# A cluster-attention and spatial-gating kernel: a greedy order of instructions replaced by a fixed list for each engine

## The chip, the cores and the metric

The kernel runs on one core of one Trainium2 chip. The metric is the device time of one execution in microseconds (us), lower is better. Three runs of the kernel before took 635.9, 635.97 and 636.34 us; the median is 635.97.

A core has five engines that run side by side, each in its own program order: TensorE (PE in the rows; its weight loads are PEld), VectorE (DVE), ScalarE (ACT), GpSimd (POOL) and SyncE (SP), which issues most of the DMAs. An engine that waits for a semaphore holds up everything behind it in its own program; so the order in which the program lists the instructions of one engine is a decision of the kernel.

## The reference

Attention over four batches of eight heads, 768 positions of width 64, where a query sees only the keys of its own cluster, and then a gated MLP per batch:

```
q_assign = argmax(normalised q . normalised centroids)      # 16 clusters per head
k_assign = argmax(normalised k . normalised centroids)
scores   = where(q_assign == k_assign, q.k / 8, -1e9)
x        = softmax(scores) . v                              # 4 x 768 x 512
h        = relu(x @ w_in);  u, v = halves of h
v_n      = (v - mean) / sqrt(var + 1e-6)
v_s      = w_spatial @ v_n + b_spatial
out      = (u * v_s) @ w_out                                # 4 x 768 x 512
```

All of it is in float32; the kernel splits each float32 into a high and a low float16 and adds products of the parts.

## The kernel before, in words

**The work.** Heads are taken two at a time: 16 pairs n, four to a batch. For each pair, `prep` loads keys and queries (`raw`, L914) and values (`vraw`, L915), makes the high part on ACT (L918) and the low part `lo` on POOL after a scaled copy on ACT (L921, L922, pairs 1 to 3) or on DVE (L924), copies parts by DMA (L925, L926, L953), multiplies with the centroids on TensorE (the logits, L940 to L942) and finds the cluster by five DVE steps (L970 to L974); ACT writes the one-hot rows `ohx` (L983), a DMA transposes them (L987) and four DMAs put them into the operands (L999). `shifts` finds each query's largest score by nine score chunks on TensorE (L1041) and nine reductions on DVE (L1048), and writes the shift into the operands: by DMA (L1066, ACT L1067 and L1073, DMAs L1095 and L1096), or for the very first head through TensorE (L1083) and a DVE addition (L1089). `attend` makes scores (L1219, L1221), exponentials on ACT (L1226), a float16 cast (ACT L1241) and its remainder (POOL L1242), and sums values on TensorE (L1248). For eight of the heads (`turned`) the probabilities are transposed by DMA (L1163) before TensorE uses them (L1170 to L1172): 6 per head, 48 in all. Pair 0 has its own `prep0` (L834 to L890) with the row casts L890 shared by DVE and ACT. `raw` has one buffer: the load for a pair can be issued only when the low part of the pair before it has been made.

`mlp` runs once per batch: products in sub-groups of six matmuls of 512 columns (L1320), named V, U, S (spatial) and O (output). From S to O lead DVE L1397, ACT L1398, POOL L1399, a DMA transpose L1400; the output goes out by ACT L1417 and a DMA from ACT's queue (L1418). There are 24 such tiles. The weights are split in between (DVE L715, L730 to L732).

**The order.** Nothing is emitted where it is written. Every operation is recorded by `op` (L323) with its engine, an estimated cost and what it needs; `Plan.run` (L345) then plays a clock forward. Before the change it kept for each engine the operations whose inputs were done, took the engine that could start first, and on it the ready operation with the smallest due time; the due times, one number for each of 3355 operations, come from the table `STARTS` (L177). So an operation that is not ready in the planner's clock never stands in the way of one that is. What comes out is a fixed program for each engine.

```
                k = o.key if o.key >= FILLER else (g if o.due is None else o.due) + o.key
                if pick is None or (k, o.seq) < pick[:2]:
                    pick = (k, o.seq, o)
```

Of the kernel before, what the change touches and what calls it, by code (L numbers as in the profile page):

```python
# [17 lines left out]
P = 128  # L18
# [16 lines left out]
FILLER = 1e6  # L35
# [58 lines left out]
K_EXP = 17.89  # L94
# [34 lines left out]
K_FILL = -8.0  # L129
# [48 lines left out]
    "c-jrqgJK<65CG7bYs`z<v`K2)wr$(CZQHhO+qP}n_U`$IQx}>7K_bWiF(3urgea_xS@8!r2!hoR3eh1LqCq%>fB_G&Apmh;9lk_hiCJz|mt9B8LRfs(ktb!DSvxj>O=I!cHnx^MWAB;d6Int&fjwux*guw<$K<hi"  # L178
    "9$uVR;vab%UYNJ!ZFvvAnvda``Dgx{2aCx(u85`jsLiaF=*n}6vLdm#$2-eHVhHcgXN$h#vS=i3i^TH2xFjx!Qu3wPEQ-j+^0)XVmdobyh)kvS%S$q~DlJdQqN<hZuDYm!YKPh``>DZdh}x(&t8Qwm+Nt)a9_p^z"
    "rZ%Z9YL~jD52|Xg8!WbfmM{^@V0=UX$OU<!5EO+n5CM_EKtWZA1@#~uw1zgY7_Q<B<e;HERDjA*3+g}$NC*~ULNmw?W1ukHgGVq9Hoyaz0`0IDHisx^3vr<n#E15f06IfT=ntu&7o>sFkO?M0R>%okU?-G<>QE52"  # L180
    "!w#qfO&||+hhi`Y%E1sQ4x^w7jE9;q6KcR5XaKXI5iEf9a23wOMR*2bPy~`dGDr?3AuUvdvak>az-vei86gW~hHOwDYC}gD3?pDT41~!r9p*wqXbf*5E+)Xeun!KvE;s>);5ZzHvv3T~z-hP!=ioBjhD&fAPC{Sk"
    "15Y3b-$7IS0PXP$v_-_hsBt&~4#hB>jG;IOqvKNi4fU`I?uR>&9$P_9>;@&U2aJVAcnAAI9ejZmus77ip->fv!6fK|Pw+2vf!xpm@<BT&03~1~C@c+Af$$c527&2t8Z3q9umoPgN_YyNU=wt}pRfl8;9B?yYv3Pj"
    "1daxez%U$yiQxhyg&U9_?!!aK0c-Iw<cGuf7@y*6d<iMpABYFv;V4{zQ?MNF!aC>*0d%+(=fgZ$1S?<_Y=v!b5Prc|cmZ$VB;Lej@Bq`XaHiQmjKt&^4^v@m%#O)0GbX`&m=OzOCM<w?usmkN7B~@8V?wNjyRjhV"
    "!u(hr>tX|}ggvl6_QlpX1V`XVoQ2bI5>CK4$XS3L!5f$cJtoEwOpC!7150CLjD<C@6&Aw?%#AUz945t-*c`iIPiTV+uo*7HuDA_P<9?h02XHygh76bm^Wq3r4F_UF?2esr9CpM`xE}A~DBO#Wa4z=7`8Wnw;uKtk"
    "SMV9$$IUnz&)`%%i}P>^KEw}r5Z~ZO{Ef(nwPc-HC$<@m<9lHE4FpJ(PzwKIaSUTCa33DR6L<|<Vj)a~MX)Ru#gdo<YvVi2&yJyCbJ!xb7<=Ms9FMzjCT_xMcoY}nDcp(Ya1UO@9e4{b;XT}rYw$KkvQPLNgV-<p"
    "iQh3fi@_4H=qwqF&C;;KEC<WVO0d#wAv?m(vSDl<dxfdlTg<?|VnJ4fDYgj9GtV~QAFRS0tIi~=!y2);Yzt;%pRoY@f+g7xEXyjhSgZl7#uBh*tPAVQ2DAM9153|VuzYMiE6R4TeXIuS#m=xcY#=Mn4zUXCC~L|t"
    "u&b;a8^p%5RxB^;z{;>5tQ@Pv#<In%9-F~-u?=h^yT*dqVfKlI<2cqI$6^(%i0^R?i-y5GAxpw?vRbSy3uTN6R*Yp~X;~(AjNN4CSP0L})A6pXKdZ@7vBoS9Yr?X#)~pa~&nmKxtSTGInzP}oA)Cv(vwkcli(ucd"
    "6kE!cu_f#T+r)OW1MCL7!d|jd>;b#YzA(na_#5_z)n*s)GIE}Zk7j+?bk>_qWj)y#wv%0FQ`kXvhb>^E*h)5=tz$FUe0H8aVlUWU_K}@rKiFlacqo6uG>_zeSsb2-C*jF?C;pS&W58dr-|RIrJir~#z@zgho`rvB"
    "#F5A4g2&@&c`}}j7vV8@5Rc8H@x(j<Ps%g#`aBKK$(!=LyeKchck;p9@-n;uFUUKIq2eaL&FAvwyaPv}L<|ukqKh~pkw_>`@-sZMc*TG5y5bT4#0!gtqNRu?a*Imh6u-h7i;iNP_$h=8l?h}jnMLN8Ib<1GRaTTy"
# [118 lines left out]
class Plan:  # L308
# [36 lines left out]
    def run(self):  # L345
# [11 lines left out]
        for o in self.ops:  # L357
# [6 lines left out]
        wait = {e: [] for e in LAG}  # L364
        hw = [0.0, FIRST]
        count, nxt, fetch = 0, FETCH[0], []
        lanes = []
# [3 lines left out]
        def arm(o):  # L371
            o.ready = max([o.at] + [a.end + lag(a, o.eng) for a in o.after] + [a.s for a in o.order])
            wait[o.eng].append(o)
# [1118 lines left out]
```

## Time and profile before

| what | value |
| --- | --- |
| median of three runs | 635.97 us |
| the profiled execution: its span from the first to the last instruction | 633.5 us |
| what the median has beyond that span | 2.5 us |
| TensorE busy | 607.2 us, 96% of the span |
| VectorE, ScalarE, GpSimd busy | 409.4, 462.7, 440.1 us |
| mean granted TensorE clock | 0.989 |

The profile gives the profiled execution's time as its span; what lies around the span is not split further, and the table takes it as the difference to the median. Busy time is an average over stages with different limits: the stages have to be read one at a time. "nm<-acc" means that the instruction reads tile acc and writes tile nm; "x5" that five like it are merged; a bracket gives the idle time before an instruction and what ended it.

### The profile page before, as it was taken

The page shows a single profiled execution, that of the slowest core. Times are in us where ns is not written, and L with a number is a line of the kernel's source. Part 1 is how long each engine was busy: PE and PEld are TensorE (multiplying, and loading weights), DVE is VectorE, ACT ScalarE, POOL GpSimd, SP SyncE. Part 2 cuts the span into 40 slices and gives each one's busy share as a digit, 9 for nine tenths or more (in the row PEclk, how much of TensorE's full clock was granted, in tenths as well). Part 3 has the DMA queues.
Part 4 walks back from the last instruction along what each step waited for, and adds up shares of the span by engine and source line. Part 5 has one row for each costly group of instructions (what it writes and reads, how often), then busy time and mean ns, then how long its engine had stood idle before and what let it go on. Part 6 is the DMA issues. An engine that isn't in the chain of part 4 may idle for free.

```text
span 633.5 us, 16596 instructions
## 1 busy us (share of the span) xinstructions
PE 607.2 (96%) x6603; PEld 371.9 (59%) x6603; DVE 409.4 (65%) x856; ACT 462.7 (73%) x842; POOL 440.1 (69%) x377
## 2 busy tenths in 40 slices
PE   2799999999999999999999999999999999999997
PEld 1466777776666665456556655575556655444443
DVE  6969999998999978457777475478733551132110
ACT  5589999998998996539887978698877984133212
POOL 3386998988998995429988875588799966144120
PEclk9879999999999999999999999999999999999999
DMA  6467988966857748722899679995995199213133
GB/s 182 135 145 141 199 172 191 213 152 141 180 97 174 155 99 201 145 74 69 179 179 215 122 185 167 146 174 86 163 190 97 30 193 171 60 35 83 41 69 106
DMA packets 175171, 87.97 MB, mean 139 GB/s; under 512 B 159315, under 2 KB 162422, under 8 KB 175094
## 3 DMA queue, kind: packets, MB, share of 16 engines
q1 hardware_dynamic: 171350, 80.24, 63.1%
q10 hardware_dynamic: 3744, 6.69, 3.2%
q8 instruction: 51, 0.84, 0.6%
q14 instruction: 26, 0.21, 0.1%
HBM read 27.66 MB, written 6.29 MB: 54 GB/s over the span
## 4 chain that ended last, share of the span: by engine, by line
PE 73%; DVE 8%; ACT 7%; DMA 5%; POOL 3%; issue 3%; SPq 0%; ACTq 0%; POOLq 0%; DVEq 0%
PE acc L1320 39%; PE acc L1248 11%; PE acc L1219 5%; PE acc L1221 5%; PE acc L1041 5%; DVE nm L1048 3%; PE acc L1123 2%; PE acc L1121 2%; DMA pt<-pt 2%; DVE lo L924 1%; POOL pt L1162 1%; ACT p L1226 1%; ACT p L1152 1%; DMA raw<-in_kqT_dram 1%; PE acc L1170 1%
## 5 line engine op out<-in xcount | busy, mean ns | idle before, releaser
L1242 POOL TENSOR_TENSOR pt<-p,pt 128x768 f16<-128x768 f32 x136 | 226.4, 1686 | 34.2 <-ACT pt L1241 27.8
L1048 DVE TENSOR_REDUCE nm<-acc 128x1 f32<-128x512 f32 (+1 forms) x216 | 137.4, 681 | 13.2 <-PE acc L1041 12.7
L1226 ACT ACTIVATE p<-acc 128x512 f32<-128x512 f32 x216 | 120.7, 603 | 21.9 <-PE acc L1221 10.4
L1320 PE MATMUL acc<-win,xT 128*128 128x512 f16 x576 | 134.8, 379 | 0.3 <-ACT p L1152 0.3
L1241 ACT CAST pt<-p 128x768 f16<-128x768 f32 x136 | 110.4, 838 | 5.5 <-PE acc L1248 2.5
L1320 PE MATMUL acc<-vn,wsp 128*128 128x512 f16 x432 | 100.1, 379 | 0.4 <-ACT p L1152 0.4
L1162 POOL TENSOR_TENSOR pt<-p,pt 128x768 f16<-128x768 f32 x48 | 80.5, 1684 | 23.5 <-ACT pt L1161 17.5
L1248 PEld LDWEIGHTS <-pt 128*128 128x128 f16 x2448 | 87.5, 98 | 14.2 <-POOL pt L1242 1.5
L1248 PE MATMUL acc<-vhl,pt 128*128 128x65 f16 x2448 | 92.9, 193 | 1.0 <-POOL pt L1242 1.0
L1320 PEld LDWEIGHTS <-xT 128*128 128x128 f16 x576 | 54.4, 97 | 60.7 <-issue 0.8
L1219 PE MATMUL acc<-hq,lo 128*128 128x512 f16 (+1 forms) x288 | 84.0, 333 | 1.8 <-ACT p L1226 0.8
L1221 PE MATMUL acc<-hq 81*128 81x512 f16 (+1 forms) x288 | 84.2, 333 | 0.0
L1041 PE MATMUL acc<-hq 80*128 80x256 f16 (+1 forms) x288 | 71.8, 335 | 4.1 <-DVE nm L1048 1.6
L1320 PEld LDWEIGHTS <-wsp 128*128 128x128 f16 x432 | 41.1, 98 | 47.2 <-issue 0.9
L1152 ACT ACTIVATE p<-acc,bi,sl 128x512 f32<-128x512 f32 (+1 forms) x96 | 58.7, 679 | 10.6 <-DVE bi L1144 6.0
L1131 DVE TENSOR_REDUCE nm<-acc 128x1 f32<-128x512 f32 (+1 forms) x72 | 47.0, 684 | 23.0 <-PE acc L1123 22.8
L1399 POOL TENSOR_TENSOR ghl<-u,ghl 128x512 f16<-128x512 f32 x21 | 25.0, 1189 | 51.0 <-ACT ghl L1398 49.0
L1397 DVE SCALAR_TENSOR_TENSOR u<-acc,bsp,u 128x512 f32<-128x512 f32 x24 | 18.0, 749 | 65.5 <-PE acc L1320 65.3
L1320 PE MATMUL acc<-wou,gT 128*128 128x512 f16 x252 | 59.3, 379 | 0.5 <-ACT ohx L983 0.5
L1297 POOL TENSOR_TENSOR xhl<-xn,xhl 128x384 f16<-128x384 f32 x32 | 33.1, 1035 | 15.2 <-ACT xhl L1296 13.3
L1161 ACT CAST pt<-p 128x768 f16<-128x768 f32 x48 | 39.8, 840 | 4.1 <-DMA wraw<-pt 2.0
L1219 PEld LDWEIGHTS <-lo 128*128 128x128 f16 x288 | 28.0, 100 | 23.8 <-issue 4.0
(162 smaller groups left out, 1010.0 us busy)
## 6 DMA issues: line engine op xcount, KB each, us to landing
raw<-in_kqT_dram SPq DMA_DIRECT2D x15, 768.0 KB
vraw<-in_vp_dram SPq DMA_DIRECT2D x16, 384.0 KB
hq<-hq SPq DMA_DIRECT2D x15, 384.0 KB
out_dram<-o ACTq DMA_DIRECT2D x21, 256.0 KB
vn<-in_w_in_dram SPq DMA_DIRECT2D x8, 512.0 KB
hq<-lo SPq DMA_DIRECT2D x15, 192.0 KB
lo<-hq SPq DMA_DIRECT2D x15, 192.0 KB
wraw<-in_wsT_dram SPq DMA_DIRECT2D x12, 192.0 KB
```

The costliest lines, as they stand in the source:

```text
L1041: T.matmul(out=acc.t[:, c:c + cs.stop - cs.start], lhsT=hq.t[0:R_SH, 1, h, t * P:(t + 1) * P], rhs=hq.t[0:R_SH, 0, h, cs], start=c == 0, s ...
L1048: V.tensor_reduce(out=nm.t[:, t, k:k + 1] if n == 1 else nm.t[:, t:t + n, k], in_=src, axis=AX.X, op=ALU.max, negate=True)
L1131: V.tensor_reduce(out=nm.t[:, t, k:k + 1] if n_ == 1 else nm.t[:, t:t + n_, k], in_=src, axis=AX.X, op=ALU.max, negate=True)
L1152: A.activation(out=p32[j].t[:, halves[x]], in_=sc.t[:, j * (S - 512):(j + 1) * (S - 512)] if x else sc.t, func=AF.Exp, bias=bi.t[:, t:t + ...
L1162: c = op("POOL", 1.64, lambda pt=pt, j=j, p32=p32: G_.tensor_tensor(out=pt.t[:, S:], in0=p32[j].t, in1=pt.t[:, 0:S], op=ALU.subtract), aft ...
L1219: T.matmul(out=o, lhsT=lo.t[:, h, ks], rhs=hq.t[:, 2, h, cs], start=x == 0, stop=False, skip_group_check=True)
L1221: T.matmul(out=o, lhsT=hq.t[0:R_E, 0, h, ks], rhs=hq.t[0:R_E, 1, h, cs], start=False, stop=True, skip_group_check=True)
L1226: o = op("ACT", 0.6, lambda: A.activation(out=p32[j0].t[:, cs] if n_ == 1 else both(p32)[:, :, cs], in_=sc.t if n_ == 1 else sc.t.rearrang ...
L1241: o = op("DVE" if fast else "ACT", C_CAST if fast else 0.83, lambda pt=pt, p32t=p32t, fast=fast: (V.tensor_copy if fast else A.copy)(out=p ...
L1242: o = op("POOL", 1.64, lambda pt=pt, p32t=p32t: G_.tensor_tensor(out=pt.t[:, S:], in0=p32t(), in1=pt.t[:, 0:S], op=ALU.subtract), after=[o ...
L1248: T.matmul(out=a[:, c * W:c * W + w], lhsT=lhsT, rhs=rhs, skip_group_check=True, **f)
L1320: T.matmul(out=acc.t[:, 0:w], lhsT=lr[m][0], rhs=lr[m][1], start=(m == 0), stop=(m == n - 1))
```

## The change

The table `STARTS` is replaced, and with it what its numbers mean. The new one, unpacked, holds for every operation its place in its engine's list: 0 to 947 on TensorE, and in the same way for 867 operations on ACT, 837 on DVE, 361 on POOL and 342 on SP. `Plan.run` sorts each engine's operations by that number and only ever looks at the first of each list:

```
-            for e, q in wait.items():
-                first = None
-                for o in q:
-                    g = gate(o)
...
+        order = {e: sorted((o for o in self.ops if o.eng == e), key=lambda o: -o.due) for e in LAG}
+            for e, q in order.items():
+                if q and not q[-1].left:
+                    g = gate(q[-1])
+                    if g is not None and (best is None or max(g, free[e]) < best[0]):
+                        best = (max(g, free[e]), e)
...
-            wait[e].remove(o)
+            o = order[e].pop()
```

Five estimated costs change with it: the fill of two constants on DVE 1.2 to 0.42 (L636, the memsets of L633 and L634), two memset groups on POOL 2.0 to 0.8 (L641) and 0.8 to 0.4 (L644), and the exponentials of turned heads 0.6 and 0.4 to 0.78 and 0.57 (L1154). The operations, their operands and their number are unchanged.

By place, 832 of TensorE's 948 operations stand elsewhere (by 4.5 places in the mean), 760 of ACT's 867, 726 of DVE's 837, 251 of POOL's 361 and 289 of SP's 342. Unpacked, the start of the new lists against the old (h0 and h1 are the two heads of a pair, z0 and z1 the two parts of a row):

```
ACT old: ... L890 p0 h1z0, L918 p1 x2, L921 p1 x2, L890 h1z1, L775 v1, L815, L781 v1, L1067, L1073, L1067, L1073,
         L815, L918 p2, L983 x2, L1226, L921 p2, L918 p2, L1226, L921 p2, L1226, L1067, L1073, L1241, L1226 x3, ...
ACT new: ... L872 x2, L918 p1 x2, L921 p1 x2, L840, L775 v1, L890 h0z1, L890 h1z0, L1067, L890 h1z1, L1073, L815,
         L781 v1, L1067, L1073, L1226, L983 x2, L918 p2, L921 p2, L918 p2, L921 p2, L1226 x2, L1241, L1226 x2, ...
SP old:  L627, L628, L828 h1, L829, L841 h0, L842 h0, L841 h1, L914 p1, L842 h1, L857 h0, L915 p1, L857 h1, L925 p1,
         L817, L915 p2, L914 p2, L926 p1, ...
SP new:  L627, L828 h1, L628, L829, L914 p1, L842 h0, L915 p1, L857 h0, L925 p1, L842 h1, L841 h0, L914 p2, L817,
         L926 p1, L841 h1, L915 p2, L857 h1, ...
DVE new: ... L656, L839 h0, L839 h1, L669 x2, L633, L865, ... L1048 x3, L890 h1 x2, L1048 x3, L1066, L1048 x2, L970 c1,
         L1089, L971, L1066, L972, L973, L974, L816, L1048 x2, L1089, L1048 x6, L970 c2, ...
PE new:  ... the nine L1041 of head 0, the logits of pair 1, L1083, L1041 x2, the first L1219/L1221, ...
```

Two later places, and the end:

```
ACT near 86 us, old:  L1226, L1226, L1241, L1226, L775 v2, L1241, L1067, L1073, L781 v2, L1226, L1226, L1296, ...
ACT there, new:       L1226, L1226, L1241, L1226, L1226, L1241, L775 v2, L1067, L781 v2, L1226, L1226, L1296, ...
DVE near 180 us, old: L1294, L1048 x4, L924 p9, L715, L1048 x2, L924 p9, L1048 x4, ...
DVE there, new:       L1048 x2, L715, L924 p9, L1293, L1048 x2, L924 p9, L1048 x2, L1294, L1048, L715, L1048 x3, ...
PE at the end, old: S35 S35 S35 O31 O31 O34 O32 O34 O32 O33 O33 O35 O35
PE at the end, new: S35 O31 O31 S35 S35 O32 O32 O33 O33 O34 O34 O35 O35
```

## Rows read from the trace of the kernel before

**Rows 1.** The page: the span, and the chain that ended last, by engine

```profile
span 633.5 us, 16596 instructions
...
PE 73%; DVE 8%; ACT 7%; DMA 5%; POOL 3%; issue 3%; SPq 0%; ACTq 0%; POOLq 0%; DVEq 0%
```

**Rows 2.** Busy time by stage: from:to, length, engines, PEclk, DMA share, GB/s

```profile
0.00:20.00 20.00, 8.18 (x71) 5.33 (x72) 13.51 (x55) 12.61 (x22) 6.70 (x25) 1.00 0.57 163
20.00:30.00 10.00, 7.11 (x71) 4.62 (x70) 9.84 (x20) 3.05 (x9) 3.61 (x3) 0.83 0.52 162
30.00:40.00 10.00, 8.37 (x74) 5.20 (x74) 5.15 (x11) 9.88 (x21) 7.25 (x5) 0.51 0.55 116
40.00:150.00 110.00, 106.97 (x1590) 80.68 (x1588) 106.22 (x199) 103.92 (x199) 95.48 (x63) 1.00 0.80 172
150.00:540.00 390.00, 386.67 (x4382) 235.28 (x4380) 258.16 (x545) 310.15 (x555) 303.98 (x250) 1.00 0.74 146
300.00:350.00 50.00, 48.87 (x516) 28.79 (x515) 37.24 (x86) 42.01 (x77) 42.85 (x40) 1.00 1.00 193
```

**Rows 3.** ACT in order of time, 29 to 43 us

```profile
29.51 0.84 ACT L918 ACTIVATE hq<-raw 128x768 f16<-128x768 f32 x1 [2.98 <-DMA raw<-in_kqT_dram]
30.26 0.53 ACT L983 ACTIVATE ohx<-acc 128x192 f16<-128x192 f32 x2
30.68 0.60 ACT L1226 ACTIVATE p<-acc 128x512 f32<-128x512 f32 x1
...
33.10 0.86 ACT L921 ACTIVATE raw<-raw 128x768 f32<-128x768 f32 x1
...
42.52 1.58 ACT L918 ACTIVATE hq<-raw 128x768 f16<-128x768 f32 x2 [0.51 <-DMA raw<-in_kqT_dram]
```

**Rows 4.** DVE in order of time, 21 to 37 us

```profile
21.61 0.15 DVE L1066 TENSOR_REDUCE nl<-nm 128x4 f32<-128x12 f32 x1
...
24.78 0.69 DVE L1089 TENSOR_TENSOR hq<-acc,hq 19x512 f16<-19x512 f32 x1
...
27.74 0.57 DVE L974 TENSOR_TENSOR acc<-acc,m 128x384 f32<-128x384 f32 x1
...
36.81 0.56 DVE L970 TENSOR_REDUCE mx<-acc 128x24 f32<-128x384 f32 x1 [4.39 <-PE acc L942]
```

**Rows 5.** POOL in order of time: the low parts of pair 1

```profile
18.75 3.24 POOL L922 TENSOR_TENSOR lo<-raw,hq 128x768 f16<-128x768 f32 x2 [5.75 <-ACT raw L921]
```

**Rows 6.** SP's queue in order of time: when DMAs were issued

```profile
9.85 0.33 SPq L914 DMA_DIRECT2D raw<-in_kqT_dram  x1
10.23 0.46 SPq L842 DMA_DIRECT2D hq<-lo  x1
...
16.03 0.46 SPq L857 DMA_DIRECT2D lo<-hq  x1
...
22.31 0.37 SPq L914 DMA_DIRECT2D raw<-in_kqT_dram  x1
...
37.37 0.36 SPq L914 DMA_DIRECT2D raw<-in_kqT_dram  x1
```

**Rows 7.** The chain that ended last, near 86 us: start, us, what

```profile
86.43 0.75 ACT wou L781
...
87.39 0.47 ACT p L1226
```

**Rows 8.** DVE in order of time, near 180 us

```profile
179.62 2.04 DVE L924 SCALAR_TENSOR_TENSOR lo<-raw,hq 128x768 f16<-128x768 f32 x1
...
182.04 1.27 DVE L1048 TENSOR_REDUCE nm<-acc 128x1 f32<-128x512 f32 x2
```

**Rows 9.** TensorE's waits after 150 us: us in total, times, longest

```profile
PE acc L1170 <- DMA wraw<-pt: 0.6, 2, 0.4
```

**Rows 10.** The end: TensorE's last matmuls and ACT's last output

```profile
623.24 6.64 PE L1320 MATMUL acc<-wou,p 128*128 128x512 f16 x30
...
630.06 0.60 ACT L1417 ACTIVATE o<-acc 128x512 f32<-128x512 f32 x1 [1.12 <-DMA out_dram<-o]
```

More of the change, by code (lines that the diff above doesn't have):

```diff
@@ L220 @@
[L220 to L222 removed]
+    "c-keH1)P*s7sgM((n~B2OLzCu-QBR%(y2&yDj^}=ASK-)5=x6oBM3-0NP~nl-+$&~emnENH%>nHoaZ89q7o_zCGbxrhPXtN=!`mlfu|70VoEG#UE(nkSBlFdnJm*~jLepbvQU=F3YjMxq^4|_9kQSA!%|-k%5QQ+cFPHgl"
@@ L363, in run @@
         free = {"PE": 0.6, "ACT": 1.1, "DVE": 0.63, "POOL": 0.57, "SP": 0.5, "NONE": 0.0}
-        wait = {e: [] for e in LAG}
         hw = [0.0, FIRST]
@@ L372, in arm @@
             o.ready = max([o.at] + [a.end + lag(a, o.eng) for a in o.after] + [a.s for a in o.order])
-            wait[o.eng].append(o)
         def gate(o):
@@ L394, in run @@
         done = 0
+        order = {e: sorted((o for o in self.ops if o.eng == e), key=lambda o: -o.due) for e in LAG}
         while done < len(self.ops):
             best = None
-            for e, q in wait.items():
-                first = None
-                for o in q:
-                    g = gate(o)
-                    if g is not None and (first is None or g < first):
-                        first = g
-                if first is not None:
-                    s = max(first, free[e])
-                    if best is None or s < best[0]:
-                        best = (s, e)
+            for e, q in order.items():
[3 more added lines that the diff above has]
+                        best = (max(g, free[e]), e)
             if best is None:
-                raise RuntimeError("the plan can't go on: " + str([(o.seq, o.eng) for q in wait.values() for o in q][:20]))
+                raise RuntimeError("the plan can't go on: " + str([(q[-1].seq, q[-1].eng) for q in order.values() if q]))
             s, e = best
-            pick = None
-            for o in wait[e]:
-                g = gate(o)
-                if g is None or g > s + 1e-9:
-                    continue
-                k = o.key if o.key >= FILLER else (g if o.due is None else o.due) + o.key
-                if pick is None or (k, o.seq) < pick[:2]:
-                    pick = (k, o.seq, o)
-            o = pick[2]
-            wait[e].remove(o)
+            o = order[e].pop()
             for tok in o.new:
@@ L634, in fill @@
         V.memset(ones, 1.0)
-    c_wt = op("DVE", 1.2, fill, key=K_FILL)
+    c_wt = op("DVE", 0.42, fill, key=K_FILL)
     c_id = op("DVE", 0.2, lambda: V.tensor_copy(out=id16, in_=idt()), after=[ld_i], use=[scratch], key=0)
@@ L1152, in ex @@
                         A.activation(out=p32[j].t[:, halves[x]], in_=sc.t[:, j * (S - 512):(j + 1) * (S - 512)] if x else sc.t, func=AF.Exp, bias=bi.t[:, t:t + 1], scale=sl.t[:, t:t + 1])
-                    e = op("ACT", (0.6, 0.4)[x], ex, after=[ys[j]], use=[sc, sl, bi] + (p32[j:j + 1] if got else []), new=[] if got else p32[j:j + 1], key=K_EXP)
+                    e = op("ACT", (0.78, 0.57)[x], ex, after=[ys[j]], use=[sc, sl, bi] + (p32[j:j + 1] if got else []), new=[] if got else p32[j:j + 1], key=K_EXP)
                     exps.append(e)
```

85 lines of the change are left out of this document (38 added, 47 removed).

## The prediction

> **What bounds the kernel now.** I read the page first, for the span and the chain that ended last. The reader is to see that TensorE is 73% of that chain and every other engine a few per cent [rows 1]: this is a TensorE kernel, and an order of instructions can win only what TensorE loses. Next comes busy time by stage, to see where it loses. In the first 40 us TensorE is busy 8.18 + 7.11 + 8.37 = 23.66 us, so it stands 16.34 us. From 40 to 150 us it stands 110 - 106.97 = 3.03 us, from 150 to 540 us 3.33 us [rows 2]. After its last matmuls, 623.24 + 6.64 = 629.88 us [rows 10], the span runs 3.6 us on [rows 1]. From 30 to 40 us the granted clock is also 0.51, about the lower of the two levels (1.2 GHz of 2.4), after a stretch of 10 us with 2.89 us of idle [rows 2]. So most of what an order can win lies before 40 us, and about 6.4 us is spread over 500. Then I read the start in order of time, engine by engine, for what each wait hangs on.
>
> **How the start loses its time.** ACT does nothing for 2.98 us until the load of pair 2 lands at 29.51 us, because its instruction L918 stands ahead of two casts of pair 1 (30.26) and of the first exponential (30.68) [rows 3]. The casts' input was ready when L974 ended, 27.74 + 0.57 = 28.3 us, and the scores' operand when the addition L1089 ended, 24.78 + 0.69 = 25.5 us [rows 4]. Pair 2's last scaled copy ends at 33.10 + 0.86 = 34.0 us [rows 3], its low part takes POOL 3.24 / 2 = 1.6 us [rows 5], and only then come its logits, for which DVE stands 4.39 us, until 36.81 [rows 4]. Everything of pair 2 hangs on that load, issued at 22.31 us, when POOL had finished the low part of pair 1 (18.75 + 3.24 = 21.99) [rows 5, 6]. The next load of the kind, issued at 37.37, ended ACT's wait at 42.52 us, so it took 5.1 us; the one of 22.31, with the values' load just ahead of it, took 7.2 us [rows 3, 6].
>
> **The change, part by part.** *The emission rule and the five costs* add and remove no instruction; they cost nothing by themselves, as the chip sees only the order that comes out. I priced the order by its places in the lists.
>
> *Start, up to the first shift.* The load of pair 1 moves ahead of two small copies on SP; it waits for the low part of pair 0, as before, was issued at 9.85 [rows 6], and can go up to 1 us earlier, as head 1's high part now stands second on ACT. The price: the copy L842 now queues behind it. The copy in that position before was issued at 10.23 and was waited for until 16.03 [rows 6], 5.8 us, so SP stands at L857 until about 9 + 5.8 = 14.8 us. Behind it stand copies that are needed only when pair 0's scores begin, after 23 us: nothing, and if that cover were gone, up to 5.8 us. The constants' fill, on DVE between two steps now, lies beside the logits on TensorE: nothing. A copy of 0.8 us (L840) before the row casts ends as they can begin: nothing. The first shift (L1066, 21.61 [rows 4]) comes at 21.3 by the same addition of DVE's steps: one row cast on ACT now stands behind pair 1's copies and gives back what DVE wins. I count 0.
>
> *Pair 1's low part* starts about 1.2 us earlier, as its two scaled copies no longer stand behind a row cast of head 1. So the load of pair 2 can go at 20.8 us instead of 22.31, and stands ahead of the values' load.
>
> *Pair 2's load and ACT's order.* The exponential and the two casts now stand ahead of L918. DVE's list after the first shift (21.3 + 0.2) is two reductions of 0.6 [rows 8], L970 at 0.56, the addition at 0.69, a small row of 0.15 and four cluster steps of 0.57 [rows 4]: 21.5 + 1.2 + 0.56 + 0.69 + 0.15 + 2.3 = 26.4 us, against 28.3. The casts (0.53) end at 27.0, and L918 can start. Its load lands at 20.8 + 5.1 = 25.9 us or, at the price of the earlier load, 20.8 + 7.2 = 28.0. The nearest row is the 5.1 one, as no other load stands ahead in either. Four copies on ACT take from 29.51 to 34.0 today with two exponentials between; without these they take 4 x 0.79 = 3.2 us (two took 1.58 [rows 3]), so they end at 30.2 (31.2) instead of 34.0. The logits, and DVE at L970, come 3.8 (2.8) us earlier. I take **3.8 us**. What is late next is the exponentials behind those four copies: the second comes near 30.2.
>
> The Trainium skill (DMA: Bandwidth & Descriptors, Queues, rings and completion order) says that on each DMA engine one queue's descriptors are consumed in ring order. By it a load put first does not share with the one behind it, and the 3.8 stands rather than 2.8; the two loads of 5.1 and 7.2 us [rows 3, 6] agree.
>
> *The clock.* At 0.51 the 8.37 us of work between 30 and 40 us are 4.2 us at the full rate [rows 2]. If the full rate comes as late after the restart as today, nothing changes; if it comes earlier or later by one stretch of three or four us, TensorE gains or loses 1.7 us. I take 0 and keep both ends.
>
> The Trainium skill (TensorE: Matmul & The Clock Gate, Part 1) says that the throttled state is the default and that activity releases it. By it the slow stretch moves along with the restart, and the sum stays as it is; full rate through the whole start would make the forecast 1.7 us lower.
>
> Does the 3.8 reach the end? DVE is busy 106.22 of 110 us from 40 to 150 [rows 2], so it is nearly a second bound there. But DVE itself waits for that same load [rows 4] and starts its stretch as much earlier too, so I carry all of it.
>
> *The 6.4 us in the middle.* I read two places. Near 86 us an exponential that scores wait for stands behind a copy of values (0.75 us) and two small shift rows until 87.39 [rows 7]; the new list puts one more exponential ahead of all three, and the wait should go, about 0.9 us. Near 180 us two reductions stand behind a low part of 2.04 us on DVE, until 182.04 [rows 8]; in the new list the low part still stands ahead of two reductions, and at most a weight copy is out of the way. One place cleared and one nearly as it was: of 6.4 us I take a third, **2.0 us**; the ends are 0 and 6.4, and a loss is the last rival.
>
> *The end.* ACT's last output waits 1.12 us, until 630.06, for the output DMA of a tile that uses the same buffer [rows 10]. The new list puts another tile between the two. The last matmuls end at 629.88, so **0.2 us** goes. The last output product follows the last spatial one by six sub-groups of 6 x 6.64 / 30 = 1.3 us [rows 10], 7.8 us.
>
> **Sum.** 633.5 - 3.8 - 2.0 - 0.2 = 627.5 us of span. The median of the runs lies 636.0 - 633.5 = 2.5 us above this execution's span, which I add: **630.0 us**.
>
> **The rivals.**
> 1. *The start wins, the middle gives nothing.* For it: a list that was built from estimates clears waits that stand in the estimates, and the low part near 180 us still stands in front [rows 8]. Against: the place near 86 us. 633.5 - 3.8 + 2.5 = 632.2 us.
> 2. *No change.* DVE is the bound from 40 to 150 us [rows 2]. If the start's gain only moves DVE's waiting from before 40 us to after it, or the lists come out in effect as the old order, the time is 636.0 us. Against: 4.39 us of DVE's waiting are for the very load that moves [rows 4].
> 3. *Slower: transposes that arrive late in a fixed list.* TensorE's program reaches 48 value sums and 24 output products whose operand comes by a DMA transpose. Today that makes TensorE wait twice, 0.6 us in all, 0.4 the longest [rows 9]. From 300 to 350 us the DMA engines are busy the whole time (1.00) [rows 2], and some output products now stand some 50 places earlier. If one arrival in three is late by 0.4 us, TensorE stands 24 x 0.4 = 9.6 us: 633.5 - 4.0 + 9.6 + 2.5 = 641.6 us. It decides from about 13 late arrivals (4.0 + 1.3 = 5.3 us). Against: 0.6 us today, in that same traffic.
>
> **How the numbers follow.** A measurement of this kernel can tell about 0.2%, 1.3 us, from no change. The forecast has 0.58, the first rival 0.20, no change 0.10, the late transposes 0.12. The first two are faster: 0.78; same 0.10; slower 0.12. The range goes down to the larger ends of the terms without all of them at once (the clock's 1.7 and about 3.8 us more of the middle: 624.5) and up to 635.5, past the first rival with the load's 2.8 and a small loss; it leaves out the slower case and a part of no change.
>
> **What would show it.** Right: pair 2's L918 near 27 us with its load issued near 21 and ahead of the values; the first exponential before 26; DVE's L970 of pair 2 near 33; TensorE idle near 12 us before 40 us; no stand near 84 us of the kind at 86; the last output without a wait for a DMA. Wrong: L918 still near 29.5; DVE's idle moved past 40 us; TensorE waits on L1163's or L1400's transposes of several us; a clock of 0.5 past 40 us.

## The result, and the profile after

The changed kernel takes 630.59 us (median of 4 runs, 628.66 to 632.64) against 635.93 for the kernel before on the same chip (634.04 to 636.34): a ratio of 0.9917, 95% interval 0.9899 to 0.9935. The forecast was 630.0. The time is as predicted; most of the reasons are not, as the experiments show, and that the sum came out is luck.

Line numbers of the new kernel are those of the kernel before less 23 (L918 is L895, L1048 is L1025); the experiments' kernels differ by a few lines more. The page of the changed kernel, to be held against [rows 1]:

```profile
span 628.8 us, 16581 instructions
...
PE 69%; DVE 9%; DMA 8%; ACT 5%; POOL 5%; issue 3%; SPq 1%; ACTq 0%; POOLq 0%; DVEq 0%
```

Busy time by stage of the changed kernel (columns as in [rows 2]):

```profile
0.00:20.00 20.00, 7.14 (x69) 4.81 (x69) 12.39 (x52) 11.22 (x19) 7.22 (x26) 1.00 0.48 147
20.00:30.00 10.00, 8.58 (x76) 5.31 (x75) 9.74 (x20) 6.31 (x16) 3.27 (x3) 1.00 0.70 194
30.00:40.00 10.00, 8.63 (x128) 5.64 (x126) 9.09 (x18) 9.94 (x21) 8.48 (x6) 1.00 0.68 180
40.00:150.00 110.00, 106.30 (x1561) 79.87 (x1560) 106.18 (x200) 103.93 (x202) 96.62 (x64) 1.00 0.79 168
150.00:540.00 390.00, 386.70 (x4388) 235.61 (x4385) 253.89 (x544) 308.88 (x550) 301.35 (x249) 1.00 0.73 145
```

The span is 4.7 us shorter, yet TensorE's idle hardly moves: 15.65 us before 40 us (16.34 in [rows 2]), 3.70 to 150 us (3.03), 3.30 to 540 us (3.33). The reader is to see that idle is the wrong measure here: a matmul at half clock counts as busy for longer, and so does one whose successor comes a little late. From 30 to 40 us TensorE is busy 8.63 us in place of 8.37 and does 128 matmuls in place of 74.

So I use another measure below, **TensorE's lag** at a time t: t less the work done by then, where each matmul begun before t counts with the usual distance to the next one of its kind at full rate (in the kernel before past 45 us, the median for 512 columns is 0.216 us, for 256 columns 0.109, for 64 and 65 columns 0.03). Two kernels with the same matmuls differ at the end by the difference of their lags. Another grouping of the matmuls moves the values by several us and differences between kernels by up to 0.8. Worked out from the traces, us:

```
at                  45    80   100   150   340   400   540 us
before            26.6  28.2  29.5  33.2  37.0  37.3  40.5
after             24.0  25.7  27.7  29.5  32.5  33.8  35.8
```

Of the 4.7 us, 2.6 stand at 45 us, 1.1 more are won by 150 us and 1.0 behind it. That is what the prediction said in kind (3.8 of the start, 2.0 of the middle), and it is the reading that the experiments overturn. A lag is that of one execution, and executions differ: at 45 us five traces with the old start (before, e2, e7, e8, e9 below) lie between about 25 and 27 us, seven with the new one (after, e1, e5, e6, e10 to e12) between 24.0 and 24.7. Differences of a microsecond between two lags can be chance.

The steps of the start, in order of time on SP and POOL, then ACT, then DVE, of the changed kernel [rows 3 to 6]:

```profile
18.38 3.24 POOL L899 TENSOR_TENSOR lo<-raw,hq 128x768 f16<-128x768 f32 x2 [6.18 <-ACT raw L898]
21.64 0.34 SPq L891 DMA_DIRECT2D raw<-in_kqT_dram  x1
22.77 0.15 DVE L1043 TENSOR_REDUCE nl<-nm 128x4 f32<-128x12 f32 x1
26.32 0.58 ACT L1203 ACTIVATE p<-acc 128x512 f32<-128x512 f32 x1
27.78 0.55 ACT L960 ACTIVATE ohx<-acc 128x192 f16<-128x192 f32 x2 [0.88 <-DVE acc L951]
28.22 0.84 ACT L895 ACTIVATE hq<-raw 128x768 f16<-128x768 f32 x1
34.46 0.56 DVE L947 TENSOR_REDUCE mx<-acc 128x24 f32<-128x384 f32 x1 [0.57 <-ACT p L1203]
```

Pair 2's load goes 0.67 us earlier (21.64, [rows 6] 22.31), ACT has no wait of 2.98 us for it any more, and pair 2's cluster step L947 comes at 34.46 in place of 36.81, 2.35 us earlier [rows 4]. The other traces show less: in the six others with the new start the load goes at 22.11 to 22.36, no earlier than before, and L947 comes at 35.02 to 35.19; in the four others with the old start it comes at 35.71 to 37.02. By the medians (35.04 and 36.81) the start wins 1.8 us there.

The chain that ended last, near 80 us, and the end, TensorE and ACT in order of time [rows 7, 10]:

```profile
78.86 2.30 DVE lo L901
...
82.28 2.30 DVE lo L901
```

```profile
622.55 2.75 PE L1297 MATMUL acc<-wou,p 128*128 128x512 f16 x12
...
625.34 0.60 ACT L1394 ACTIVATE o<-acc 128x512 f32<-128x512 f32 x1 [1.35 <-PE acc L1297]
```

At 86 us the exponential no longer stands behind copies; two low parts of 2.30 us on DVE stand in the chain in its place. At the end the last output waits for TensorE (625.30) and not for a DMA.

### The profile page after: what moved, and what is told of

It reads as the page before. It is cut to its first block, busy times and chain, and to the rows that moved or that the text cites. A ratio compares the mean times of both kernels' runs of the same rounds, so it can differ in the third digit from the quotient of the medians.

```text
span 628.8 us, 16581 instructions
## 1 busy us (share of the span) xinstructions
PE 602.7 (96%) x6603; PEld 369.7 (59%) x6603; DVE 404.2 (64%) x856; ACT 462.6 (74%) x842; POOL 439.1 (70%) x377
## 4 chain that ended last, share of the span: by engine, by line
PE 69%; DVE 9%; DMA 8%; ACT 5%; POOL 5%; issue 3%; SPq 1%; ACTq 0%; POOLq 0%; DVEq 0%
PE acc L1297 39%; PE acc L1225 9%; PE acc L1196 4%; PE acc L1198 4%; PE acc L1018 4%; DVE nm L1025 3%; POOL pt L1139 2%; PE acc L1100 2%; PE acc L1098 2%; DMA hq<-oht 2%; DMA sht<-shx 1%; POOL pt L1219 1%; ACT p L1203 1%; DVE lo L901 1%; PE acc L1148 1%
## 5 line engine op out<-in xcount | busy, mean ns | idle before, releaser
L1025 DVE TENSOR_REDUCE nm<-acc 128x1 f32<-128x512 f32 (+1 forms) x216 | 140.2, 680 | 29.0 <-PE acc L1018 27.7
L1203 ACT ACTIVATE p<-acc 128x512 f32<-128x512 f32 x216 | 122.8, 603 | 19.1 <-PE acc L1198 8.9
L1196 PE MATMUL acc<-hq,lo 128*128 128x512 f16 (+1 forms) x288 | 82.4, 326 | 2.5 <-ACT p L1203 1.2
L1198 PE MATMUL acc<-hq 81*128 81x512 f16 (+1 forms) x288 | 82.5, 327 | 0.8 <-DMA hq<-sht 0.4
L1018 PE MATMUL acc<-hq 80*128 80x512 f16 (+1 forms) x288 | 75.5, 336 | 4.8 <-DVE hq L867 1.3
L1129 ACT ACTIVATE p<-acc,bi,sl 128x512 f32<-128x512 f32 (+1 forms) x96 | 60.5, 676 | 14.9 <-DVE bi L1121 12.1
L1108 DVE TENSOR_REDUCE nm<-acc 128x1 f32<-128x512 f32 (+1 forms) x72 | 47.2, 683 | 24.0 <-PE acc L1100 23.8
L1018 PEld LDWEIGHTS <-hq 80*128 80x128 f16 x288 | 27.0, 101 | 23.3 <-issue 4.1
L1297 PEld LDWEIGHTS <-gT 128*128 128x128 f16 x252 | 24.1, 98 | 27.2
```

What stands on the lines that cost most here:

```text
L1018: T.matmul(out=acc.t[:, c:c + cs.stop - cs.start], lhsT=hq.t[0:R_SH, 1, h, t * P:(t + 1) * P], rhs=hq.t[0:R_SH, 0, h, cs], start=c == 0, s ...
L1025: V.tensor_reduce(out=nm.t[:, t, k:k + 1] if n == 1 else nm.t[:, t:t + n, k], in_=src, axis=AX.X, op=ALU.max, negate=True)
L1108: V.tensor_reduce(out=nm.t[:, t, k:k + 1] if n_ == 1 else nm.t[:, t:t + n_, k], in_=src, axis=AX.X, op=ALU.max, negate=True)
L1129: A.activation(out=p32[j].t[:, halves[x]], in_=sc.t[:, j * (S - 512):(j + 1) * (S - 512)] if x else sc.t, func=AF.Exp, bias=bi.t[:, t:t + ...
L1196: T.matmul(out=o, lhsT=lo.t[:, h, ks], rhs=hq.t[:, 2, h, cs], start=x == 0, stop=False, skip_group_check=True)
L1198: T.matmul(out=o, lhsT=hq.t[0:R_E, 0, h, ks], rhs=hq.t[0:R_E, 1, h, cs], start=False, stop=True, skip_group_check=True)
```

## The experiments

The old order written as a fixed list gives the program of the kernel before (in the traces of e3 and e9 every engine has the instructions of the kernel before in the same order, apart from what these two add or replace), so the new rule and the five costs move nothing by themselves; all that differs is the place of instructions in the lists. A list can be divided in time: what began before some time in the planner's clock in one order, the rest in the other.

**1. The start alone (e1).**

```diff
-STARTS = new
+STARTS = for each engine: those that start before 45 us in the new order, in that order; then the others in the old order
```

> The new lists for the operations of the first 45 us of the plan, the old order for all that follows. If the gain is made at the start (TensorE has done some 3 us more work by 40 us in the new trace), 632.9 us against 635.9 before, with the granted clock at 1.00 from 20 to 40 us. If it is made in the middle, 635.9. If a start and a rest only work together, above 634.5.

Measured: 637.87 us, ratio 1.0042 (1.0025 to 1.0059): 0.4% slower. The lag is 24.7 us at 45 us, as it should be, and 32.7 at 80. POOL's and TensorE's waits of e1 from 45 to 75 us (us in total, times, longest):

```profile
POOL bsp L722 <- DMA bsp<-in_b_sp_dram: 3.5, 1, 3.5
...
PE acc L1224 <- POOL pt L1218: 2.8, 2, 2.3
```

and its stretch from 40 to 80 us, where the kernel before has 39.28 us of busy TensorE, x590, at 0.99:

```profile
40.00:80.00 40.00, 36.88 (x473) 27.84 (x470) 31.61 (x60) 30.70 (x61) 28.21 (x20) 0.87 0.70 139
```

At the seam a scaling on POOL (L722) came to stand ahead of its data: it waits 3.5 us for a load, the remainders `pt` behind it wait too, TensorE stands for them, and runs a part of the stretch at the lower clock (0.87 in the mean). One entry of a fixed list, some places too early, cost about 3 us: e5 below differs from e1 by its place alone and takes 634.64. It is a fault of how I joined the lists, so this run says nothing of the start.

**2. The rest alone (e2).**

```diff
-STARTS = new
+STARTS = for each engine: those that start before 45 us in the old order, in that order; then the others in the new order
```

> The other half: the old order for the first 45 us of the plan, the new lists for all that follows. If the middle is worth the 2.0 us of the prediction, 633.9 us, with the old start (clock 0.5 from 30 to 40 us, pair 2's load landing at 29.5). If all of the gain is the start, 635.9.

Measured: 630.21 us, ratio 0.9907 (0.9895 to 0.9920): all of the gain, with the old start. Its start is that of the kernel before [rows 2]:

```profile
20.00:30.00 10.00, 7.25 (x72) 4.62 (x70) 9.85 (x21) 3.04 (x9) 3.72 (x3) 0.83 0.55 164
30.00:40.00 10.00, 8.26 (x72) 5.03 (x72) 5.26 (x11) 9.91 (x20) 7.14 (x5) 0.52 0.50 107
```

The lag is 26.8 us at 45 us (before 26.6), 29.7 at 150 and 34.5 at 540. So the new lists behind 45 us win 6.0 us by themselves, 3.7 of them before 150 us, and the new start on top of them wins nothing.

**3. The clock of the start alone (e3).** The old order, with 29 more matmuls of 512 columns, whose results nobody reads, in TensorE's pauses between 10 and 36 us.

```diff
-WARM = ()
+WARM = ((2.5, 6), (4.5, 3), (17.5, 5), (29.5, 3), (30.5, 4), (32.5, 1), (33.5, 1), (34.5, 1), (35.5, 5))
```

> The old order throughout, with 29 more matmuls of 512 columns on constants, put where TensorE waits between 10 and 36 us, their results unused. Theory clock: the start's gain is that TensorE never falls to half rate; then the clock reads 1.00 from 20 to 40 us and the time falls by 2 us or more, to 634 or less, though ACT still waits for pair 2's load until 29.5 us. Theory load: the gain is the earlier load and copies of pair 2; then DVE still starts pair 2's cluster step at 36.8 us and the time stays within 0.5 us of 635.9, whatever the clock reads.

Measured: 635.93 us, ratio 0.9997 (0.9984 to 1.0011). The granted clock rose from 0.83 and 0.51 [rows 2] to

```profile
20.00:30.00 10.00, 6.84 (x73) 3.86 (x72) 9.85 (x20) 5.06 (x13) 3.66 (x3) 0.89 0.58 179
30.00:40.00 10.00, 10.00 (x86) 5.52 (x84) 3.80 (x9) 7.69 (x16) 6.82 (x5) 0.76 0.71 163
```

and the median did not move. The full rate that the expectation asked for was not reached in this trace, which is of one of the slowest of e3's twelve executions (637.55 us, mean clock 0.994). By their mean clock the twelve spread: four under 0.996 took 636.43 to 638.79 us (median 637.2), four at 0.999 and above 633.55 to 636.77 (median 634.8). So the run shows that these matmuls win nothing in the median; that the full rate through the whole start is worth nothing it does not show.

**4. Pair 2's load put back behind the values (e4).**

```diff
 SP's list
-raw of pair 2, three others, vraw of pair 2
+three others, vraw of pair 2, raw of pair 2
```

> The new lists with one instruction of SP moved: pair 2's load of keys and queries goes behind pair 2's load of values (four places later), as it stood before the change. Values can be loaded only when ACT has read pair 1's, so the load goes out near 26.5 us instead of 21.6 and lands near 32. Theory load: ACT's L895 of pair 2 starts 3.5 us later than 28.2, and the whole gain of the start goes: 633.5 to 634.5 us. Theory clock: the same only if the clock falls to 0.5 with it, and with the clock at 1.00 the time stays under 632. If the load's place does not matter, 630.6.

Measured: 634.99 us, ratio 0.9992 (0.9977 to 1.0008): nearly the whole gain is gone. L895 of pair 2 starts at 34.24 us, 6.0 later than in the changed kernel and not 3.5, so the time lies above the range of the theory of the load too. From 30 to 40 us TensorE is busy 4.57 us (8.63 in the changed kernel) at a clock of 0.83, the lag at 45 us is 30.1, at 540 us 39.3. Together with e2 this places the start: at 45 us the lags of the changed kernel, e2 and e4 are 24.0, 26.8 and 30.1; at 540 us 35.8, 34.5 and 39.3. A start that is 3.3 us later than the old one is paid in full (4.8 us at the end and in the medians of e4 and e2); one that is earlier is not paid out. The place of the load is worth much in the new lists, but what it does is to keep their start from being late.

**5. The start alone, without the fault of e1 (e5).**

```diff
 POOL's list of e1
-bsp (L722) at its old place
+bsp (L722) behind the values of pair 2
```

> The new lists for what began in the first 45 us, the old order behind, with POOL's second scaling load and scaling placed as the new lists have it, so that the 3.5 us wait of e1 falls away. Theory A (the start's lead is absorbed further on, whatever the order behind it): 635.9 plus or minus 1.2, ratio within 0.2% of 1, although the lag of TensorE at 45 us is 2.5 us less than in the kernel before. Theory B (the prediction's: the start carries its lead to the end, and it was only the seam of e1 that lost it): 632.2 to 633.5, ratio 0.994 to 0.996. Rival C (another misplaced instruction at the seam): above 637, and then a wait of over 1 us between 45 and 70 us shows which.

Measured: 634.64 us, ratio 0.9988 (0.9973 to 1.0004). The ratio is within A's 0.2%, the time 0.1 us under A's range and 1.1 above B's: A, nearly. The lag is 24.5 us at 45 us, 2.1 less than before; at 80 us 0.6 of that is left, at 540 us 1.0. The start alone is worth about 1 us, and no change at all lies inside the interval too.

**6. Where the lead goes: is it DVE's load? (e6, e7)** DVE is busy 69.3 of the 70 us from 80 to 150 us in the changed kernel, which made it the suspect. Both kernels leave out half of the columns of the row maximum for pairs 2 to 6, e6 with the new start and e7 with the old one.

```diff
 def most():
     src = acc.t if n == 1 else acc.t.rearrange("p (t c) -> p t c", t=2)
+    if 2 <= n_ <= 6:
+        src = acc.t[:, 0:256] if n == 1 else src[:, :, 0:128]
```

> The changed kernel, with VectorE's max reductions of pairs 2 to 6 taken over half of the columns (this leaves out half of the columns of the max for these pairs); it frees about 0.27 us x 18 x 5 = 24 us of VectorE between 30 and 150 us and changes no order. Together with e7, which does the same to the kernel with the old start and the new rest. Theory A1 (VectorE, 69 of 70 us busy between 80 and 150 us, is the bound that absorbs the start's lead): this one comes out 2 to 3 us under e7, near 626 to 628, as the lead of 2.5 us at 45 us is carried. Rival A2 (another thing absorbs it, such as TensorE's or ScalarE's own order): within 1 us of e7.

> The old order for what began in the first 45 us and the new lists behind it (e2), with VectorE's max reductions of pairs 2 to 6 taken over half of the columns, as in e6. Theory A1 (VectorE is the bound that absorbs the start's lead): 629 to 630.5, 2 to 3 us above e6, as the late start is no longer caught up. Rival A2: the same time as e6 within 1 us; if both are then far under 630 (by 2 us or more), VectorE did bound this stretch but the start is caught up all the same.

Measured: e6 628.20 us, ratio 0.9879 (0.9860 to 0.9899); e7 629.80, ratio 0.9911 (0.9891 to 0.9932). From 80 to 150 us DVE is busy 59.43 and 59.24 us now: some 10 us of it are free, and e7 has the time of e2 (630.21). DVE's load is not what bounds the new lists behind 45 us when the start is the old one. With the new start it may be: e6 is 2.4 us under the changed kernel (630.59), and their intervals only touch, at 0.9899. e6 is also 1.6 us under e7, on the side of A1, but there the intervals overlap, and A1 asked for 2 to 3. So A1, that DVE's work takes back the lead, is neither shown nor excluded.

**7. The old order up to 150 us, the new lists behind (e8).**

```diff
-STARTS = new
+STARTS = for each engine: those that start before 150 us in the old order, in that order; then the others in the new order
```

> The old order for all that began in the first 150 us of the model's clock, the new lists behind it. It splits the gain of the rest (5.7 us in e2) by place. By the lag of TensorE in the two traces, 3.5 us of the 5.7 are won before 150 us and about 2 behind: Theory D (won in the middle's beginning, 45 to 150 us): 634 plus or minus 0.8. Rival E (won behind 150 us, and the lag at 150 us is only moved work): 630.2 to 632. Rival F (won by 150 us alone, nothing behind): 635.5 to 636.5.

Measured: 634.46 us, ratio 0.9978 (0.9964 to 0.9993). By the medians 1.1 us of e2's 5.8 are won by the new lists behind 150 us alone, so most of it, 4.7 us, needs the new lists between 45 and 150 us. Theory D.

**8. Is it the low parts that POOL holds up? (e9, e10)** The low part `lo` on DVE takes 0.95 us when POOL does nothing, and much longer beside a POOL instruction. DVE and POOL of the kernel before, near 80 us:

```profile
79.33 1.64 POOL L1242 TENSOR_TENSOR pt<-p,pt 128x768 f16<-128x768 f32 x1 [0.45 <-ACT pt L1241]
80.40 3.71 DVE L924 SCALAR_TENSOR_TENSOR lo<-raw,hq 128x768 f16<-128x768 f32 x2
81.58 1.71 POOL L1242 TENSOR_TENSOR pt<-p,pt 128x768 f16<-128x768 f32 x1 [0.61 <-POOL pt L1242]
```

The first `lo` ends 0.82 us after POOL's first instruction (80.97), the second 0.82 us after its second (83.29 and 84.11): as if each began in earnest when POOL had ended. Between 45 and 150 us the 8 low parts take 12.2 us before, 10.5 after and 7.6 in e2; in the changed kernel the two rows of the chain above are two of them. That fitted everything: the middle's gain, and the start's lead lost at 80 us. So both kernels were run with a `lo` that reads `raw` alone, for pairs 4 to 8; it leaves out the subtraction.

```diff
+if 4 <= n <= 8:
+    los.append(op("DVE", 0.95, lambda h=h: V.tensor_reduce(out=lo.t[:, h, :], in_=raw.t[:, h, :].unsqueeze(2), axis=AX.X, op=ALU.max),
+        after=[his[h]], use=[raw, hq] + ([lo] if h else []), new=[] if h else [lo], key=KL, port=True))
+    continue
```

> The order of the kernel before, with VectorE's low halves lo of pairs 4 to 8 formed by an instruction that reads only raw (a maximum over an axis of one element, 128x768 f32 to f16) in place of raw minus hq; it leaves out the subtraction for these pairs. Theory G (in the traces so far lo runs 0.95 us alone, but where a POOL tensor_tensor is under way it ends 0.81 us after that one's end: 12.2 us for 8 between 45 and 150 us in the kernel before, 7.6 in e2; that waiting on POOL, in a stretch where VectorE is 69.9 of 70 us busy, is the middle's loss): the 8 fall to about 0.95 each, TensorE's lag grows by 2 us from 60 to 150 us in place of 5.1, and the time falls by 2.5 to 4.5 us, to 631.4 to 633.4. Rival H (the held lo's only fill time in which VectorE would have waited anyway, and the new order gains by other places): within 1 us of 635.9, or the new instruction is held as well, which its durations show.

> The changed kernel with the same replacement of lo in pairs 4 to 8 (the subtraction is left out for them). In the changed kernel two of the eight, at 78.8 and 82.3 us, are held by POOL to 2.38 and 2.30 us, 2.8 us in all, and TensorE's lag grows from 25.0 to 27.7 us just there, while in e2, where none is held, it stands at 27.7 to 28.0. Theory G (what the start wins is given back to these two held instructions, by their phase against POOL, and not to a standing bound): 627.3 to 628.6, 2 to 3 us under the changed kernel, so that the start's lead of 2.5 us comes through. Rival A1 (VectorE's sum of work absorbs the start, whoever is held): 630 to 630.6.

Measured: e9 635.85 us, ratio 0.9999 (0.9986 to 1.0012); e10 629.68, ratio 0.9908 (0.9885 to 0.9931). Theory G falls for the old order. Its own instructions came out as it said: the two of 3.71 us now take 1.80, beside the same POOL instructions, and DVE's stretch from 80 to 150 us (69.86 us busy before) has 4 us free. But DVE now waits 4.8 us for TensorE between 45 and 150 us, where it waited 1.6 before. DVE of e9 near 80 us, in order of time:

```profile
80.07 1.80 DVE L901 TENSOR_REDUCE lo<-raw 128x768 f16<-128x768 f32 x2
```

Busy time from 80 to 150 us, of the kernel before and then of e9:

```profile
80.00:150.00 70.00, 67.69 (x1003) 50.58 (x1003) 69.86 (x129) 68.14 (x130) 62.34 (x41) 1.00 0.77 173
```

```profile
80.00:150.00 70.00, 67.88 (x1008) 50.90 (x1005) 65.82 (x129) 68.00 (x130) 60.17 (x41) 1.00 0.82 173
```

DVE's waits for TensorE from 45 to 150 us, in the same order:

```profile
DVE nm L1048 <- PE acc L1041: 1.6, 3, 0.9
```

```profile
DVE nm L1027 <- PE acc L1020: 4.8, 6, 1.3
```

The lag at 150 us is 33.2 in both, and from 80 us on it grows by the same within 0.2 us. An engine that is busy 99.8% of a stretch did not bound it. The Trainium skill (Perfetto Trace Analysis, Identifying the Most-Contended Engine) takes the engine with the highest occupancy for the one to improve first, and occupancy as a fair measure for VectorE (TensorE it judges by other measures). By that rule DVE would be the engine to free in this stretch; 4 us of it freed did not show in the time, and the measurement decides.

**9. The start's lead, with one or two entries moved (e11, e12).** Nothing is left out in these two.

```diff
 DVE's list
-m31.1, lo of pair 5 first half, m30.8, m31.4, lo of pair 5 second half
+lo of pair 5 first half, m31.1, m30.8, m31.4, lo of pair 5 second half     (e11)
+lo of pair 5 first half, m31.1, m30.8, lo of pair 5 second half, m31.4     (e12)
```

> The changed kernel with one entry of VectorE's list moved: pair 5's first lo stands one place earlier, before the row maximum that preceded it, so that it should start near 78.1 us, ahead of POOL's tensor_tensor at 78.7, and the second one near 81, ahead of that at 82.1. Nothing is left out. Theory G: the two take 0.95 to 1.3 us each in place of 2.38 and 2.30, and the time falls by 1.5 to 2.8 us, to 627.8 to 629.1, which would beat both kernels. Rival A1 (a standing bound absorbs it): 630 to 630.8 although the two are short. Third outcome: another POOL instruction meets them, they are still over 2 us, and the time is that of the changed kernel.

> As e11, and pair 5's second lo one place earlier too. Theory G: the same 627.8 to 629.1 where both come out short; where one of them meets POOL it is read from their durations, and the time is higher by what it is held, up to 1.4 us each. Rival A1: 630 to 630.8 whatever their durations.

Measured: e11 630.33 us, ratio 0.9911 (0.9891 to 0.9932); e12 629.71, ratio 0.9896 (0.9877 to 0.9916). Neither can be told from the changed kernel (0.9899 to 0.9935). The lags show what happened to the lead:

```
at                  45    80   100   150   340   400   540 us
after             24.0  25.7  27.7  29.5  32.5  33.8  35.8
e2 (old start)    26.8  27.8  28.0  29.7  33.0  33.4  34.5
e10               24.5  26.0  26.1  28.5  31.3  34.0  35.0
e11               24.7  26.5  26.6  28.7  32.0  34.2  35.4
e12               24.5  25.0  25.0  28.4  31.2  33.8  34.7
```

The changed kernel leads e2 by 2.8 us at 45 us, by 2.1 at 80 and by 0.3 at 100, behind the two held low parts; in e10 to e12 they are not held long there, and 1.9, 1.4 and 3.0 us of lead are left at 100 us. So the traces bear out Theory G for this place; its time, 627.8 to 629.1, was not reached. A part of the lead goes already between 100 and 150 us: of e12's 3.0 us 1.3 are left, behind five stops of 0.28 to 0.52 us that wait for ACT or DVE at different places. By 400 us the lead is gone in all three. DVE of e12 near 80 us, in order of time:

```profile
77.50 1.41 DVE L900 SCALAR_TENSOR_TENSOR lo<-raw,hq 128x768 f16<-128x768 f32 x1
...
80.03 1.20 DVE L900 SCALAR_TENSOR_TENSOR lo<-raw,hq 128x768 f16<-128x768 f32 x1
```

And TensorE's waits of e12 between 380 and 400 us, where e2 has none:

```profile
PE acc L1146 <- DMA p<-pt: 1.4, 1, 1.4
```

e10 has the same wait of 1.4 us at the same place, e11, e6 and e7 one of 1.1 to 1.3. TensorE reaches a value sum before its operand has come through a DMA transpose, in a stretch (380 to 400 us) where the DMA engines are busy 0.99 of the time in e12 and 0.91 in e2. The changed kernel and e2, which come there later, do not have it. So 1.4 of the 2.2 us that e12 loses against e2 between 340 and 400 us stand at this matmul. That coming early is what makes the wait is not shown: e8, which comes later still, waits 1.0 us at the same matmul, and no run takes the transpose away.

## Why the prediction was right, and where it was not

**The time** came out at 630.6 for 630.0, inside the range; the sign and the mechanism in general (waits of TensorE that an order can clear) were right. The two terms that carried it were not: 3.8 for the start and 2.0 for the middle add up to 5.8 us, and e2 wins 5.8 us by the middle alone. That two errors of opposite sign cancel is luck. The span came out at 628.8 for 627.5, and the 2.5 us added to it were 1.8 (630.59 - 628.8).

**The start, 3.8 us: mis-sized, and carried to the end wrongly.** In itself it was worth 2.35 us at DVE's L947 and 2.6 us of lag at 45 us in the two traces, and 1.8 us at L947 by the medians of all. It lost against the forecast in two steps. Pair 1's low part ended 0.37 us earlier (21.62 for 21.99), not 1.2, so the load went at 21.64 and not at 20.8. And I counted 0 for the first shift, which I put at 21.3; it came at 22.77, 1.2 us later than before, so that the casts of pair 1 ran to 28.3 and not to 27.0, and L895 started behind them, at 28.22. Behind both steps stands DVE's and ACT's order in pair 0. DVE's last cluster steps of its two heads, in the kernel before:

```profile
11.59 0.35 DVE L869 TENSOR_TENSOR acc<-acc,m 128x192 f32<-128x192 f32 x1
...
13.04 0.37 DVE L869 TENSOR_TENSOR acc<-acc,m 128x192 f32<-128x192 f32 x1
```

and DVE of the changed kernel, then ACT, in order of time:

```profile
10.71 0.81 DVE L614 CAST id<-p 128x128 f16<-128x128 f32 x1
...
12.22 0.37 DVE L846 TENSOR_TENSOR acc<-acc,m 128x192 f32<-128x192 f32 x1
...
14.59 0.68 DVE L867 CAST hq<-acc 17x512 f16<-17x512 f32 x1 [0.55 <-ACT hq L867]
15.20 0.34 DVE L846 TENSOR_TENSOR acc<-acc,m 128x192 f32<-128x192 f32 x1
...
19.92 1.01 DVE L867 CAST hq<-acc 17x512 f16<-17x512 f32 x2 [0.59 <-ACT hq L817]
```

```profile
15.57 0.39 ACT L849 ACTIVATE xT<-acc 128x96 f16<-128x96 f32 x2 [1.02 <-DVE acc L846]
15.99 1.58 ACT L895 ACTIVATE hq<-raw 128x768 f16<-128x768 f32 x2
...
19.05 0.83 ACT L817 COPY hq<-hq 64x768 f16<-64x768 f16 x1
```

A cast of 0.81 us (L614) that I had not priced stands between head 0's steps, and they end 0.6 us later; head 1's last step stands behind a row cast and comes 2.2 us later (15.20 for 13.04). ACT waits 1.02 us for that step, and pair 1's copies behind it start at 15.99 (16.36 before). Later DVE's row casts wait 0.59 us for a copy (L817) that stands behind pair 1's copies; copies of this kind I had put at nothing. How much of the 1.2 us each of these makes was not tested. When pair 2's load landed is not shown: L895 found its data at 28.22 without a wait, so the load took at most 6.6 us, but with the old place it took 7.2 us before and 6.2 and 6.4 in e7 and e9. The step on ring order stays open. What failed outright is the sentence "so I carry all of it". e2 has the old start and the whole gain. I had asked where the lead could be lost and looked at one engine's load only. The traces show it lost at places: in the changed kernel 1.8 of its 2.8 us over e2 go between 80 and 100 us, behind the two held low parts; with those short, a part goes in small stops up to 150 us and 1.4 us to a transpose near 393 us. Whether DVE's work as a whole (e6) would take it back as well stays open.

**The middle, 2.0 us of 6.4: mis-sized.** The new lists behind 45 us win 6.0 us in e2's trace and 5.8 in the medians (636.03 less 630.21). I had bounded it by TensorE's idle in the view by stage, and took a third. The distance between matmuls shows more than that view. Stops of TensorE that are over 0.18 us longer than the usual distance, between 45 and 150 us, and how much the lag grows there:

```
              before   e3   e8   e9   after   e10   e11   e12   e4   e2
stops            10   10   10   11      7     5     6     7    4    2
their sum, us   4.6  4.7  4.8  5.5    4.5   2.7   3.1   2.8  1.8  1.3
lag grows, us   6.6  6.6  6.7  7.7    5.5   4.0   4.0   3.9  2.8  2.9
```

Of the four kernels with the old order there, before, e3 and e8 have the same ten stops, and e9 shares about half of them: each of the four has one of 0.98 us at 86.6 to 87.5 us and one of 0.7 us at 139.5 to 140.4. In e2 both are gone. TensorE's waits from 45 to 150 us, of the kernel before and of e2:

```profile
PE acc L1248 <- POOL pt L1242: 1.0, 3, 0.4
PE acc L1219 <- ACT p L1226: 0.8, 1, 0.8
PE acc L1041 <- DVE nm L1048: 0.8, 2, 0.6
PE acc L798 <- DVE win L715: 0.3, 1, 0.3
```

```profile
PE acc L1195 <- ACT p L1202: 0.5, 1, 0.5
PE acc L1017 <- DMA hq<-oht: 0.4, 1, 0.4
```

The reader is to see that the stops of before hang on three engines in turn. That fits with freeing one of them (e9) giving nothing, and with a list that sets all of them against each other giving much; shown by runs is only where the gain stands (e2, e8). The place near 86 us that I had read [rows 7] is one of these: the wait for ACT of 0.8 us is gone in e2, as forecast (0.9). In the changed kernel it is gone too, but TensorE stands there for two row maxima behind the held low parts (its waits from 80 to 90 us):

```profile
PE acc L1018 <- DVE nm L1025: 0.8, 1, 0.8
PE acc L917 <- DVE nm L1025: 0.7, 1, 0.7
```

Which entries of which list clear the others was not taken apart; it stays open.

**The clock, 0 us.** No run speaks against it, but none shows it. The Trainium skill (TensorE: Matmul & The Clock Gate, Part 1) calls the throttled state the default, released by activity, from which I had the slow stretch move along with the restart. It did not here: the trace of the changed kernel shows 1.00 in every stage. e3 raises the clock without a gain in the median; but within e3 the executions at the highest clock are shorter than those at the lowest, by 2.4 us, and which of the two causes the other is not shown. The end of 1.7 us that I kept (0.83 over 10 us [rows 2] is 1.7 us short of the full rate) is not excluded.

**The end, 0.2 us.** The wait for the output DMA at the last tile is gone, as forecast; a wait of 2.14 us for one stands a tile earlier, under TensorE's work. What follows TensorE's last matmul is 3.5 us for 3.6, so 0.1 us was won.

**The rivals.** The first (start wins, middle nothing) is the reverse of what was found. The second's mechanism, DVE as the bound from 40 to 150 us, is refuted by e9 in the old order and by e7 in the new one with the old start; with the new start e6 leaves it open. Its remark that the start's gain may only move waiting was right. The third, late transposes, cost the changed kernel nothing; e10 and e12 met one, 1.4 us at one place.

## What to carry to other kernels

A lead at the start is worth only what no later event takes back: before it is carried to the end, go through the places further on that hang on something else (a transfer, another engine's instruction) and ask at each how early its own input comes. A bound is not read from a busy share: measure where the bounding engine's work falls behind, by the distance between its instructions, and free the suspect by itself before believing it. In a fixed list one entry whose input comes late stops everything behind it, so an instruction that is moved forward needs the load that feeds it moved forward too. And a forecast that comes out is no proof of its terms: run each term alone.

## What the runs showed of the hardware

DVE's instructions do not all behave alike beside POOL's tensor_tensor. In five of the traces (before, after, e2, e3, e4) `lo`, which reads two tiles, has a median of 1.39 us and at most 2.43 where a POOL tensor_tensor was under way at its start (62 cases; in 57 of them it ended 0.81 to 0.82 us after POOL's instruction), and 0.95, at most 0.96, elsewhere (68). The row maximum, which reads a PSUM tile, is 0.68 us in 1190 cases of the first kind and 250 of the second, and the reduction of `raw` alone in e9 and e10 stayed at 0.93 to 0.95 beside the same instructions. POOL is held by `lo` as well: the 1.65 us of `pt` become up to 2.4. The Trainium skill (SBUF — State Buffer, SBUF: two separate sides) has the rule: a port pair of VectorE and GpSimd is locked for a whole instruction, and a VectorE instruction with two SBUF inputs takes it against a GpSimd one that reads SBUF. The trace agrees, down to the 0.82 us that `lo` still runs when POOL has ended. I had not looked for it in the prediction, where the 2.04 us of [rows 8] are such a held `lo`.

The granted clock of the start does not follow from the order alone. e5, e6, e10 and e12 have the same lists up to 45 us, save for a shorter maximum from pair 2 on in e6, and show 0.68, 1.00, 1.00 and 0.69 from 20 to 30 us; the kernel before shows 0.83, and e8, with the same start, 1.00. The lags of the four at 45 us are 24.5 to 24.7 us all the same.
